# Two blocks of attention on one core: A's tokens transposed by DMA, weights on a second queue, eight heads accumulated at once

## The chip, the core and the metric

The kernel runs on one core of one Trainium2 chip. The metric is the time of one execution on the device in microseconds; where several executions are compared, their median. TensorE multiplies, VectorE and ScalarE read its results from PSUM (eight banks of 128 x 2 KB) and compute on them, GpSimd does small sums, and SyncE does nothing but issue DMAs. ScalarE can issue DMAs too; its queue is another one than SyncE's. In the profile, PE is TensorE's matmul, PEld its weight load, DVE VectorE, ACT ScalarE, POOL GpSimd, SP SyncE; a q behind an engine's name means its sequencer.

## The reference

Two independent problems A and B of the same shape, whose results stand side by side in the output. Each projects 16 x 32 tokens to 32 query heads, lets each group of eight heads attend to one of four cached key/value heads of 512 positions, and projects back:

```python
B, Sq, D = 16, 32, 1024
Hq, Hkv, Sk, Dh = 32, 4, 512, 128
q = (x @ wq).reshape(B, Sq, Hq, Dh).transpose(0, 2, 1, 3)
k = jnp.repeat(k_cache, Hq // Hkv, axis=1)
v = jnp.repeat(v_cache, Hq // Hkv, axis=1)
scores = jnp.einsum("bhqd,bhkd->bhqk", q, k) * (Dh ** -0.5)
o = jnp.einsum("bhqk,bhkd->bhqd", softmax(scores), v)
out = o.transpose(0, 2, 1, 3).reshape(B, Sq, Hq * Dh) @ wo
```

All inputs and outputs are bf16. x is 512 tokens by 1024, that is 1 MB; wq and wo are 8 MB each, and the keys and the values 8 MB each, for each problem.

## The kernel before

The kernel has a fast path, which holds all the time measured here, and a general path that is entered only when a check of the softmax sums fails. The fast path's order is written out by hand (a manual schedule): the program text gives the order on every engine and queue, and the framework adds the waits.

Everything follows 128 slots. A slot i is one pair of batch and key/value head: `scores(i)` (L357) makes four matmuls of a transposed key tile with eight heads' queries and an exponential on ScalarE, `partial_sums(i)` (L377) sums on VectorE, and five slots later `values(i)` (L424) multiplies with V and `normalize` (L438) writes the result. Between these TensorE works off `units` (L579), a stream of single matmuls: the query projections `q_units` (L299) of A's heads 8 to 31 and of all of B's, then the output projections `f_units` (L320). Each slot takes six or seven units.

The loads are issued by SyncE's queue in the order of the program. `load_k(j)` (L273) brings K for four slots as transposed tiles kT, with four DMA transposes of 128 KB for A and one of 512 KB for B; `load_v(j)` (L286) brings V for the same slots in one DMA of 512 KB; `load_wq(pr, c4)` (L246) brings the query weights of four heads, 1 MB, into a tile that it enters under (pr, c4) in the table `wq_tiles`, from which `q_units` takes it when a head begins. A plan (L583 to L603) says at which slot each load is issued. For the query weights it reads:

```python
for c4 in range(3, 16):
    need = (c4 - 2) * 4 * DC / 7.0
    at(max(0, int(need) - 10), load_wq, c4 // 8, c4 % 8)
```

so the tiles 3 and 4 are issued at slot 0, tile 5 at slot 3. At most eight DMAs of the two queues are outstanding on their eight semaphores: an issue waits for the DMA that used its semaphore before.

Ahead of the slots lies the projection of A's first eight heads, the part that the change is about (L460 to L561). SyncE loads x in five DMAs (`load_x`, tokens on partitions) and the weights of eight heads in eleven (`load_w0`), in turn. `transpose_x(k)` (L506) lets TensorE transpose two 128-column chunks of x through PSUM, and VectorE and ScalarE copy them to `xT`. `first_head` (L525) is one matmul of one head and one chunk of 128 columns. Six heads are accumulated chunk by chunk in six PSUM banks while the other two banks take the transposes; then the last two heads follow, each with its eight chunks in a row. `evacuate` (L534) copies a head to `qT`. A few matmuls on a zero tile (`warm_up`, L498) fill the time until the first data arrive. Behind them in SyncE's queue stand kT(0)'s first tile, wq(0,2), the rest of kT(0), V(0), kT(1) and V(1) (L489 to L494).

Of the kernel before, what the change touches and what calls it, by code (L numbers as in the profile page):

```python
# [8 lines left out]
BF16 = mybir.dt.bfloat16  # L9
FP32 = mybir.dt.float32  # L10
# [6 lines left out]
P = 128  # L17
HQ = 32
DH = 128
HKV = 4  # L20
REP = HQ // HKV
QD = 32
HALF = REP // 2
# [158 lines left out]
def kernel(  # L182
# [14 lines left out]
    nc = tc.nc  # L197
    B, SQ, D = A_x.shape
    SK = A_k_cache.shape[2]
    NTOK = B * SQ  # L200
    DC = D // P
    KC = SK // P
    TT = NTOK // P
    NOUT = D
    NW = 512
    NH = NOUT // NW
    GRP = 4
# [10 lines left out]
    def fast_path(ok_i):  # L218
        with ExitStack() as fctx:
            enter = fctx.enter_context  # L220
            const = enter(tc.tile_pool(name="const", bufs=1))
# [4 lines left out]
            psum = enter(tc.tile_pool(name="psum", bufs=2, space=bass.MemoryType.PSUM))  # L226
            enter(tc.manual_schedule())

            nc.scalar.preload_act_table_set("natural_log_exp_and_others")


            warm = work.tile([P, P], BF16, name="warm", tag="p_sb", bufs=7)
            nc.vector.memset(warm[:], 0.0)
            ident = const.tile([P, P], BF16, name="ident")
            make_identity(nc, ident[:])
            shift = const.tile([P, 1], FP32, name="shift")
            nc.vector.memset(shift[:], SHIFT)
            rall = const.tile([P, NG // 2, GRP * REP], FP32, name="rall")
# [2 lines left out]
            def blk_tile(shape, name, dtype=BF16):  # L241
                return blk.tile(shape, dtype, name=name, tag="blk")
# [3 lines left out]
            def load_wq(pr, c4, eng=None, parts=((0, 4),)):  # L246
                t = blk_tile([P, DC, 4 * DH], "wq_sb")
                v = problems[pr][3].rearrange("(c p) n -> p c n", p=P)
                for a, b in parts:
                    (eng or nc.sync).dma_start(  # L250
                        out=t[:, :, a * DH:b * DH],
                        in_=v[:, :, (c4 * 4 + a) * DH:(c4 * 4 + b) * DH],
                    )
                wq_tiles[pr, c4] = t
# [10 lines left out]
            def kv_part(j, which):  # L265
                pr, jj = divmod(j, NG // GRP)
                t = problems[pr][which]
                if pr == 0:
                    g, b0 = divmod(jj * GRP, B)
                    return t[b0:b0 + GRP, g]  # L270
                return t[jj]

            def load_k(j, qs=slice(0, GRP)):  # L273
                ks = kv_part(j, 1)
                if qs.start == 0:
                    k_tiles[j] = kv.tile([P, GRP, SK], BF16, name="kT")
                kT = k_tiles[j]
                if j < NG // GRP:
                    for q in range(qs.start, qs.stop):
                        nc.sync.dma_start_transpose(out=kT[:, q, :], in_=ks[q])  # L280
                else:
                    nc.sync.dma_start_transpose(
                        out=kT[:], in_=ks.rearrange("g k d -> (g k) d")
                    )

            def load_v(j):  # L286
                v_sb = v_tiles[j] = kv.tile([P, GRP, KC, DH], BF16, name="v_sb")
                nc.sync.dma_start(  # L288
                    out=v_sb[:],
                    in_=kv_part(j, 2).rearrange("q (p c) d -> p q c d", c=KC),  # L290
                )


            xT = [None, None]
            qT = {}
# [126 lines left out]
            ob = {}  # L422
# [34 lines left out]
                )  # L457


            x_sb = blk_tile([P, TT, D], "x_sb")  # L460
            x_v = A_x.flatten_outer_dims().rearrange("(t p) d -> p t d", p=P)
            wq_v = A_wq.rearrange("(c p) n -> p c n", p=P)
            HC = DC // 2
            w0 = [blk_tile([P, HC, REP * DH], "w0_sb") for _ in range(2)]

            def load_x(k, ts=slice(0, TT)):
                cs = slice(2 * k * P, (2 * k + 2) * P)
                nc.sync.dma_start(out=x_sb[:, ts, cs], in_=x_v[:, ts, cs])  # L468

            def load_w0(dcs, ns):  # L470
                nc.sync.dma_start(  # L471
                    out=w0[dcs.start // HC][:, dcs.start % HC:(dcs.stop - 1) % HC + 1, ns],
                    in_=wq_v[:, dcs, ns],
                )

            NF = REP - 2
            early, late = slice(0, NF * DH), slice(NF * DH, REP * DH)
            load_x(0, slice(0, TT // 2))
            load_x(0, slice(TT // 2, TT))
            load_w0(slice(0, 1), slice(0, NF * DH // 2))  # L480
            load_w0(slice(0, 1), slice(NF * DH // 2, NF * DH))
            load_w0(slice(1, 2), early)
            for k in range(1, DC // 2):
                load_x(k)
                load_w0(slice(2 * k, 2 * k + 1), early)
                load_w0(slice(2 * k + 1, 2 * k + 2), early)
            for half in (slice(0, HC), slice(HC, DC)):
                load_w0(half, late)
            load_k(0, slice(0, 1))  # L489
            load_wq(0, 2)  # L490
            load_k(0, slice(1, GRP))
            load_v(0)
            load_k(1)
            load_v(1)  # L494

            warm_ps = psum.tile([P, NW], FP32, name="warm_ps", tag="proj")

            def warm_up(n):  # L498
                for _ in range(n):
                    nc.tensor.matmul(  # L500
                        warm_ps[:, 0:P], lhsT=warm[:], rhs=warm[:], start=True, stop=True
                    )

            xT[0] = blk_tile([P, DC, NTOK], "xT")

            def transpose_x(k, fill=(0, 0)):  # L506
                ps = [
                    psum.tile([P, NTOK], BF16, name="xT_ps", tag="ob") for _ in range(2)
                ]
                for n, ts in zip(fill, (range(0, TT // 2), range(TT // 2, TT))):  # L510
                    for o in range(2):
                        dc = 2 * k + o
                        for tt in ts:
                            nc.tensor.transpose(  # L514
                                ps[o][:, tt * P:(tt + 1) * P],
                                x_sb[:, tt, dc * P:(dc + 1) * P],
                                ident[:],
                            )
                    warm_up(n)
                nc.vector.tensor_copy(out=xT[0][:, 2 * k, :], in_=ps[0][:])  # L520
                nc.scalar.copy(out=xT[0][:, 2 * k + 1, :], in_=ps[1][:])

            qT[0, 0] = blk_tile([P, B, REP, SQ], "qT")

            def first_head(q_ps, h, dc):  # L525
                nc.tensor.matmul(  # L526
                    q_ps,
                    lhsT=w0[dc // HC][:, dc % HC, h * DH:(h + 1) * DH],
                    rhs=xT[0][:, dc, :],
                    start=(dc == 0),  # L530
                    stop=(dc == DC - 1),
                )

            def evacuate(q_ps, h):  # L534
                copy = nc.vector.tensor_copy if h in (2, 1, 5, 7) else nc.scalar.copy
                copy(
                    out=qT[0, 0][:, :, h, :],
                    in_=q_ps.rearrange("p (b s) -> p b s", s=SQ),
                )

            warm_up(19)
            transpose_x(0, (2, 4))
            first_q = []
            for _ in range(2):
                pair_ps = psum.tile([P, 2, NW], FP32, name="q_ps", tag="s")
                first_q += [pair_ps[:, k, :] for k in range(2)]
            first_q += [psum.tile([P, NW], FP32, name="q_ps", tag="proj")[:] for _ in range(2)]
            for dc in range(DC - 2):
                for h in range(NF):
                    if dc % 2 and h == NF // 2:  # L550
                        transpose_x(dc // 2 + 1)
                    first_head(first_q[h], h, dc)
            for h in (0, 2, 4, 1, 3, 5):
                for dc in (DC - 2, DC - 1):
                    first_head(first_q[h], h, dc)
                evacuate(first_q[h], h)
            for h in range(NF, REP):
                q_ps = psum.tile([P, NW], FP32, name="q_ps", tag="ob")
                for dc in range(DC):
                    first_head(q_ps[:], h, dc)  # L560
                evacuate(q_ps[:], h)  # L561

            def stream():
                for h in range(REP, HQ):
# [20 lines left out]
            def at(slot, fn, *args):  # L585
                plan.setdefault(slot, []).append((fn, args))

            for j in range(2, 2 * NG // GRP):
                at(GRP * (j - 1), load_k, j)
                at(GRP * (j - 1) + 2, load_v, j)  # L590
            for c4 in range(3, 16):
                need = (c4 - 2) * 4 * DC / 7.0
                at(max(0, int(need) - 10), load_wq, c4 // 8, c4 % 8)
# [108 lines left out]
```

## Time and profile before

| | us |
|---|---|
| median of 14 runs | 346.93 |
| lowest and highest | 346.22, 348.57 |
| the profiled execution | 346.59 |
| its span, from first to last instruction | 344.8 |
| PE busy | 336.2 (98%) |
| DVE busy | 267.2 (78%) |
| ACT busy | 187.1 (54%) |
| A's first eight heads, first matmul to the next stage's first | 4.66 to 20.35 |
| first score matmul | 21.43 |

The granted TensorE clock is at full speed in all 40 slices of the span. The DMA engines moved 71.70 MB, 208 GB/s in the mean; 85% of sixteen engines' time went to SyncE's queue. A busy share is an average over stages, and a matmul's busy time includes what is pipelined under its neighbours, so the 98% of PE say little about a single stage; the chain of waits and the rows of single stretches do. A line of the chain gives a start, a length, and the engine and line, or the transfer, in which the time went. A line of a windows view gives a stretch, its length, for each engine the busy time and the number of instructions, then the granted clock, the share of the sixteen DMA engines (over 1 where packets of one engine overlap), and GB/s.

### The profile page before, as it was taken

What the parts mean: (1) busy time and instruction counts of PE and PEld (TensorE: products, weight loads), DVE (VectorE), ACT (ScalarE), POOL (GpSimd) and SP (SyncE); (2) the same over time, 40 slices, a digit from 0 to 9 for tenths busy, and PEclk for the clock granted to TensorE, in tenths of its full rate; (3) what the DMA queues carried; (4) which work ended last, traced back from release to release, by engine and by line L of the source; (5) the groups of instructions that cost most, each with busy time, mean ns of one, the idle gap of its engine ahead of it and who ended that gap; (6) DMA issues with size and microseconds to landing.
All of it is one profiled execution on the core that took longest, in us unless ns stands there. A gap on an engine that the chain in (4) does not pass through costs nothing.

```text
span 344.8 us, 5491 instructions
## 1 busy us (share of the span) xinstructions
PE 336.2 (98%) x2098; PEld 213.8 (62%) x2137; DVE 267.2 (78%) x338; ACT 187.1 (54%) x210; POOL 46.7 (14%) x206
## 2 busy tenths in 40 slices
PE   8997999999999999999999999999999999999996
PEld 5554666666666666666666666666666666666555
DVE  1236888888988898888888898889888888888540
ACT  2346667666676667666654545554455555554010
POOL 0001100111111111111002212221222100111100
PEclk9999999999999999999999999999999999999999
DMA  6999989899999988999999956999749997460001
GB/s 186 315 173 336 240 238 274 169 282 242 281 260 225 230 230 235 215 246 278 287 273 237 242 139 164 338 261 216 131 113 302 330 188 158 91 124 0 17 18 33
DMA packets 126509, 71.70 MB, mean 208 GB/s; under 512 B 73744, under 2 KB 126224, under 8 KB 126480
## 3 DMA queue, kind: packets, MB, share of 16 engines
q1 hardware_dynamic: 125952, 70.20, 85.3%
q0 software_dynamic: 384, 1.05, 0.8%
q8 instruction: 17, 0.28, 0.4%
q14 instruction: 12, 0.10, 0.1%
q10 hardware_dynamic: 144, 0.07, 0.1%
HBM read 51.38 MB, written 2.10 MB: 155 GB/s over the span
## 4 chain that ended last, share of the span: by engine, by line
PE 89%; SPq 5%; DMA 3%; issue 1%; ACT 0%; ACTq 0%
PE f_ps L325 31%; PE q_ps L306 25%; PE ob L430 17%; PE s_ps L362 16%; SPq L280 4%; DMA wq_sb<-in_A_wq_dram 2%; DMA x_sb<-in_A_x_dram 1%; SPq L471 1%; SPq L468 0%; SPq L288 0%; SPq L250 0%; ACT o_sb L334 0%; SPq L697 0%; ACTq L334 0%
## 5 line engine op out<-in xcount | busy, mean ns | idle before, releaser
L370 ACT ACTIVATE p_sb<-s_ps,shift 128x1024 bf16<-128x1024 f32 x128 | 142.7, 1115 | 103.3 <-PE s_ps L362 85.5
L381 DVE TRANSPOSE_TENSOR_REDUCE parts<-p_sb 128x32 f32<-128x1024 bf16 x128 | 158.9, 1242 | 20.8 <-ACT p_sb L370 19.1
L325 PE MATMUL f_ps<-wo_sb,oT 128*128 128x512 bf16 (+1 forms) x525 | 127.5, 366 | 0.5
L306 PE MATMUL q_ps<-xT,wq_sb 128*128 128x512 bf16 x430 | 113.7, 379 | 2.4 <-DMA wq_sb<-in_A_wq_dram 1.9
L430 PE MATMUL ob<-p_sb,v_sb 128*128 128x256 bf16 x512 | 76.8, 273 | 0.8
L362 PE MATMUL s_ps<-qT,kT 128*128 128x256 bf16 x512 | 76.8, 273 | 0.0
L325 PEld LDWEIGHTS <-oT 128*128 128x128 bf16 x544 | 53.2, 98 | 36.0
L362 PEld LDWEIGHTS <-kT 128*128 128x128 bf16 x512 | 56.8, 113 | 28.4 <-issue 0.3
L306 PEld LDWEIGHTS <-wq_sb 128*128 128x128 bf16 x448 | 43.7, 98 | 33.6 <-DMA wq_sb<-in_A_wq_dram 2.1
L430 PEld LDWEIGHTS <-v_sb 128*128 128x128 bf16 x512 | 50.1, 98 | 20.0
L452 DVE TENSOR_TENSOR oT<-r,ob 128x512 bf16<-128x512 f32 x64 | 43.9, 686 | 23.2 <-PE ob L430 22.7
L416 DVE STREAM_TRANSPOSE r<-rall 128x512 f32<-128x512 f32 x64 | 44.2, 691 | 1.1
L314 ACT CAST qT<-q_ps 128x512 bf16<-128x512 f32 x56 | 32.7, 583 | 13.8 <-PE q_ps L306 13.8
L399 POOL COPY half<-cs 64x32 f32<-64x32 f32 x32 | 6.5, 204 | 230.8 <-DVE cs L389 230.8
L334 ACT CAST o_sb<-f_ps 128x512 bf16<-128x512 f32 (+1 forms) x17 | 9.5, 559 | 24.4 <-PE f_ps L325 16.7
L526 PE MATMUL q_ps<-xT,w_sb 128*128 128x512 bf16 x62 | 14.4, 379 | 0.5 <-DVE xT L520 0.2
L389 DVE TENSOR_REDUCE cs<-parts 128x32 f32<-128x128 f32 x32 | 12.0, 376 | 1.1
L411 DVE RECIPROCAL rall<-sums 128x32 f32<-128x32 f32 x32 | 10.2, 320 | 1.6 <-POOL sums L408 1.6
L526 PEld LDWEIGHTS <-w_sb 128*128 128x128 bf16 x64 | 6.0, 98 | 7.4 <-DMA w_sb<-in_A_wq_dram 0.6
L520 DVE COPY xT<-xT_ps 128x512 bf16<-128x512 bf16 x4 | 1.7, 424 | 11.4 <-PE xT_ps L514 11.4
L336 POOL DMA_DIRECT2D out_dram<-o_sb x8 | 4.6, 574 | 33.2 <-ACT o_sb L334 33.1
L400 POOL TENSOR_TENSOR half<-half,cs 64x32 f32<-64x32 f32 x32 | 7.8, 243 | 2.6
(26 smaller groups left out, 50.8 us busy)
## 6 DMA issues: line engine op xcount, KB each, us to landing
v_sb<-in_A_v_cache_dram SPq DMA_DIRECT2D x16, 512.0 KB, 4.6
wq_sb<-in_B_wq_dram SPq DMA_DIRECT2D x8, 1024.0 KB, 6.3
wo_sb<-in_A_wo_dram SPq DMA_DIRECT2D x8, 1024.0 KB, 7.2
v_sb<-in_B_v_cache_dram SPq DMA_DIRECT2D x16, 512.0 KB, 4.7
wo_sb<-in_B_wo_dram SPq DMA_DIRECT2D x8, 1024.0 KB, 8.5
wq_sb<-in_A_wq_dram SPq DMA_DIRECT2D x6, 1024.0 KB, 7.6
w_sb<-in_A_wq_dram SPq DMA_DIRECT2D x7, 192.0 KB, 4.8
kT<-in_A_k_cache_dram SPq DMA_TRANSPOSE x64, 4.5
```

The source lines that it names most:

```text
L280: nc.sync.dma_start_transpose(out=kT[:, q, :], in_=ks[q])
L306: nc.tensor.matmul(ps[:], lhsT=w[:, dc, (h % 4) * DH:(h % 4 + 1) * DH], rhs=xT[pr][:, dc, :], start=(dc == 0), stop=(dc == DC - 1),)
L314: nc.scalar.copy(out=qT[pr, g][:, :, hl, :], in_=ps[:].rearrange("p (b s) -> p b s", s=SQ),)
L325: nc.tensor.matmul(ps[:, 0:width], lhsT=oT[pr, tt][:, h, :], rhs=wo_tiles[pr, nh, h // REP][:, h % REP, off:off + width], start=(h == 0), ...
L362: nc.tensor.matmul(s_ps[:, c, :], lhsT=kT[:, i % GRP, c, :], rhs=qT[pr, g][:, b, :, :].rearrange("p h s -> p (h s)"), start=True, stop=True,)
L370: nc.scalar.activation(out=p_sb[:], in_=s_ps[:], func=ACTF.Exp, bias=shift[:], scale=SCALE)
L381: nc.vector.tensor_reduce(out=parts[k][:, q, :, :].rearrange("p c h -> p (c h)"), in_=st[i]["p"][:].rearrange("p c (h s) -> p (c h) s", s=SQ),
L389: nc.vector.tensor_reduce(out=cs[:], in_=parts.pop(k)[:].rearrange("p q c h -> p q h c"), axis=AX.X, op=ALU.add,)
L416: nc.vector.transpose(out=r[:].rearrange("p n s -> p (n s)"), in_=rall[:, k, o * 2 * REP:(o + 1) * 2 * REP] .unsqueeze(2).to_broadcast([P, ...
L430: nc.tensor.matmul(ob[j][:, q, :], lhsT=v_sb[:, i % GRP, c, :], rhs=st[i]["p"][:, c, :], start=(c == 0), stop=(c == KC - 1),)
L452: nc.vector.tensor_tensor(out=out, in0=rcp.pop(j)[:].rearrange("p (q h) s -> p q h s", h=REP), in1=ob.pop(j)[:].rearrange("p q (h s) -> p ...
L526: nc.tensor.matmul(q_ps, lhsT=w0[dc // HC][:, dc % HC, h * DH:(h + 1) * DH], rhs=xT[0][:, dc, :], start=(dc == 0), stop=(dc == DC - 1),)
```

## The change

- x of A is no longer loaded and transposed on TensorE: SyncE issues five DMA transposes that write `xT` directly, two of one 128-column chunk and three of two chunks.
- The weights of the first eight heads are loaded from ScalarE's queue in six DMAs, the last three of 512 KB each; wq(0,2) is issued there too, and ScalarE's table load stands behind them.
- All eight heads are accumulated chunk by chunk, in all eight PSUM banks; the last two chunks are done head by head, and VectorE and ScalarE copy the heads in turn.
- SyncE's queue holds, behind x: kT(0), wq(0,3), kT(1), V(0), V(1). The plan of the slots is unchanged for the weights (it starts at tile 3).
- V's tiles 2 to 5 are loaded in two halves each.
- The identity, the transposes, their copies and the x tile are gone; there are 22 warm-up matmuls in a row instead of 25 in three groups.

```diff
-            nc.scalar.preload_act_table_set("natural_log_exp_and_others")
-            ident = const.tile([P, P], BF16, name="ident")
-            make_identity(nc, ident[:])
...
-            def load_v(j):
+            def load_v(j, pieces=1):
                 v_sb = v_tiles[j] = kv.tile([P, GRP, KC, DH], BF16, name="v_sb")
...
+                v = kv_part(j, 2).rearrange("q (p c) d -> p q c d", c=KC)
+                for k in range(pieces):
+                    qs = slice(k * GRP // pieces, (k + 1) * GRP // pieces)
+                    nc.sync.dma_start(out=v_sb[:, qs], in_=v[:, qs])
...
+            def load_x(d0, d1):
+                nc.sync.dma_start_transpose(
+                    out=xT[0][:, d0:d1, :],
+                    in_=A_x.flatten_outer_dims()[:, d0 * P:d1 * P],
+                )
+
+            def load_w0(d0, d1, h0=0, h1=REP):
+                nc.scalar.dma_start(
+                    out=w0[d0 // HC][:, d0 % HC:(d1 - 1) % HC + 1, h0 * DH:h1 * DH],
+                    in_=wq_v[:, d0:d1, h0 * DH:h1 * DH],
+                )
+
+            load_x(0, 1)
+            load_w0(0, 1, 0, HALF)
+            load_w0(0, 1, HALF, REP)
+            load_x(1, 2)
+            load_w0(1, 2)
+            for d0 in range(2, DC, 2):
+                load_x(d0, d0 + 2)
+                load_w0(d0, d0 + 2)
+            load_wq(0, 2, nc.scalar)
+            nc.scalar.preload_act_table_set("natural_log_exp_and_others")
+            load_k(0)
+            load_wq(0, 3)
+            load_k(1)
             load_v(0)
-            load_k(1)
             load_v(1)
...
+            first_q = [psum.tile([P, NW], FP32, name="q_ps", tag="proj")[:] for _ in range(2)]
+            for _ in range(2):
+                pair_ps = psum.tile([P, 2, NW], FP32, name="q_ps", tag="s")
+                first_q += [pair_ps[:, k, :] for k in range(2)]
+            first_q += [psum.tile([P, NW], FP32, name="q_ps", tag="ob")[:] for _ in range(2)]
+
+            for _ in range(22):
...
+            for dc in range(DC - 2):
+                for h in range(REP):
+                    first_head(h, dc)
+            for n, h in enumerate((2, 4, 0, 3, 1, 5, 6, 7)):
+                for dc in (DC - 2, DC - 1):
+                    first_head(h, dc)
+                copy = nc.vector.tensor_copy if n % 2 else nc.scalar.copy
...
-                at(GRP * (j - 1) + 2, load_v, j)
+                at(GRP * (j - 1) + 2, load_v, j, 2 if j < 6 else 1)
```

More of the change, by code (lines that the diff above doesn't have):

```diff
@@ L284, in load_k @@
                     )
-            def load_v(j):
+            def load_v(j, pieces=1):
                 v_sb = v_tiles[j] = kv.tile([P, GRP, KC, DH], BF16, name="v_sb")
[L288 to L291, printed above, removed]
+                v = kv_part(j, 2).rearrange("q (p c) d -> p q c d", c=KC)
+                for k in range(pieces):
+                    qs = slice(k * GRP // pieces, (k + 1) * GRP // pieces)
+                    nc.sync.dma_start(out=v_sb[:, qs], in_=v[:, qs])
             xT = [None, None]
@@ L457, in normalize @@
                 )
-            x_sb = blk_tile([P, TT, D], "x_sb")
-            x_v = A_x.flatten_outer_dims().rearrange("(t p) d -> p t d", p=P)
-            wq_v = A_wq.rearrange("(c p) n -> p c n", p=P)
+            xT[0] = blk_tile([P, DC, NTOK], "xT")
+            qT[0, 0] = blk_tile([P, B, REP, SQ], "qT")
             HC = DC // 2
             w0 = [blk_tile([P, HC, REP * DH], "w0_sb") for _ in range(2)]
-            def load_x(k, ts=slice(0, TT)):
-                cs = slice(2 * k * P, (2 * k + 2) * P)
-                nc.sync.dma_start(out=x_sb[:, ts, cs], in_=x_v[:, ts, cs])
@@ L470, in load_w0 @@
[L470 to L473, printed above, removed]
-                )
[L476 to L491, printed above, removed]
+            wq_v = A_wq.rearrange("(c p) n -> p c n", p=P)
+            def load_x(d0, d1):
+                nc.sync.dma_start_transpose(
+                    out=xT[0][:, d0:d1, :],
+                    in_=A_x.flatten_outer_dims()[:, d0 * P:d1 * P],
+                )
@@ L492, in fast_path @@
+            load_wq(0, 2, nc.scalar)
[3 more added lines that the diff above has]
+            load_k(1)
             load_v(0)
-            load_k(1)
             load_v(1)
[L496 to L527, printed above, removed]
+            first_q = [psum.tile([P, NW], FP32, name="q_ps", tag="proj")[:] for _ in range(2)]
[3 more added lines that the diff above has]
+            first_q += [psum.tile([P, NW], FP32, name="q_ps", tag="ob")[:] for _ in range(2)]
@@ L528, in first_head @@
+            for _ in range(22):
+                nc.tensor.matmul(
+                    first_q[REP - 1][:, 0:P], lhsT=warm[:], rhs=warm[:], start=True, stop=True
+                )
+            def first_head(h, dc):
+                nc.tensor.matmul(
+                    first_q[h],
                     lhsT=w0[dc // HC][:, dc % HC, h * DH:(h + 1) * DH],
@@ L532, in first_head @@
                 )
-            def evacuate(q_ps, h):
-                copy = nc.vector.tensor_copy if h in (2, 1, 5, 7) else nc.scalar.copy
+            for dc in range(DC - 2):
[5 more added lines that the diff above has]
+                copy = nc.vector.tensor_copy if n % 2 else nc.scalar.copy
                 copy(
                     out=qT[0, 0][:, :, h, :],
-                    in_=q_ps.rearrange("p (b s) -> p b s", s=SQ),
+                    in_=first_q[h].rearrange("p (b s) -> p b s", s=SQ),
                 )
[L541 to L561, printed above, removed]
             def stream():
```

## The prediction

> **What bounds the kernel now.** I read the page first, then the waits of TensorE, the chain of waits up to 36 us, and the DMA windows of the first 31 us. The page's chain says that TensorE sets the time, but not everywhere:
>
> ```profile
> PE 89%; SPq 5%; DMA 3%; issue 1%; ACT 0%; ACTq 0%
> PE f_ps L325 31%; PE q_ps L306 25%; PE ob L430 17%; PE s_ps L362 16%; SPq L280 4%; DMA wq_sb<-in_A_wq_dram 2%; DMA x_sb<-in_A_x_dram 1%; SPq L471 1%; SPq L468 0%; SPq L288 0%; SPq L250 0%; ACT o_sb L334 0%; SPq L697 0%; ACTq L334 0%
> ```
>
> The 8% of queue and transfer lie at the start. TensorE's waits in the whole span are these three:
>
> ```profile
> PE q_ps L306 <- DMA wq_sb<-in_A_wq_dram: 1.9, 1, 1.9
> PE warm_ps L500 <- DVE shift L237: 1.1, 1, 1.1
> PE q_ps L526 <- DVE xT L520: 0.2, 1, 0.2
> ```
>
> So after the start there is one stall, 1.87 us, for a weight tile. The chain (start us, us, what) tells which:
>
> ```profile
> 4.82 4.76 DMA x_sb<-in_A_x_dram
> ...
> 9.59 1.32 SPq L280
> ...
> 22.54 1.26 SPq L280
> ...
> 24.47 6.96 DMA wq_sb<-in_A_wq_dram
> ...
> 31.48 1.69 PE q_ps L306 x7
> ```
>
> It is wq(0,3), the weights of heads 12 to 15: issued at 24.47, landed at 31.43, awaited by TensorE since 29.6. Before 31.43 the chain holds no TensorE work at all. It runs back through SyncE's queue: K's transposes, V, the first loads. After it TensorE has no other wait to the end. The end of the kernel therefore follows the landing of wq(0,3) one for one, and whatever happens in the first projection counts only as far as it moves that landing, or outlasts it.
>
> **The first projection, TensorE's side.** In before it runs from 4.66 to 20.35, 15.69 us: 64 matmuls at a spacing of 0.218 (L306 x7: 1.69 less the last one's 0.379, over six) are 14.0; 24 token transposes at 0.057 (eight in 0.62, the last 0.219) are 1.4; waits the rest. The change takes all 32 transposes off TensorE, with their eight PSUM copies (0.42 on VectorE, 0.59 on ScalarE) and the identity on GpSimd, which ran beside other work. The new first matmul needs x's first transposed chunk. Its nearest row is kT, the same 512x128 bf16: 2.8 us from issue to landing at the least, 5.2 in the median. From 0.86 that is 3.7 to 6.1; I take 4.2, since nothing but weights is queued ahead. The stage then ends at 4.2 + 14.0 = 18.2 (17.7 to 20.1), 2.2 us before 20.35. The later chunks come in time: a kT issue takes 1.26 to 1.32 on SyncE's queue, a pair of chunks some 1.7 (B's xT: 6.79 for eight), so the last pair is issued by about 9 and its matmuls start at 4.2 + 6 x 1.74 = 14.6.
>
> ScalarE issues seven loads at 0.43 to 0.58 and then its 1.28 us table load; the last load waits for x's chunks 4 and 5 (landing near 9), so all is over near 11, and the first PSUM copy is wanted near 15. Cost nothing; without that cover, a delay of ScalarE's copies. Of the copies in alternation (0.59 and 0.69 per 0.87 us of matmuls) none is late; the pairs that share a tile have 0.28 us to spare. Scores still start 1.08 us after the stage's last matmul. The shorter queue of warm-up matmuls (22 for 25) is hidden under the wait for the first loads.
>
> Unstalled, TensorE would ask for wq(0,3) at 18.2 + 9.25 = 27.4 (9.25 is 20.35 to 29.6). In before it asked at 29.6 and got it at 31.43. So the 2.2 us gained arrive in front of the same door. What opens it?
>
> **The door: bytes ahead of wq(0,3).** The instruction order of the changed kernel shows wq(0,3) loaded twice: once behind kT(0), once in slot 0, where the plan still starts at 3. The second load replaces the tile in the table, and heads 12 to 15 read the second one; no matmul reads the first. SyncE's queue now holds x, kT(0), the unread copy, kT(1), v(0), v(1), and only then the copy that is read. In before 7.3 MB land ahead of and with wq(0,3) (x 1, weights of eight heads 2, wq(0,2) 1, two kT, two v, itself 1, in 1.05 MB units); now 8.4 MB. The DMA rows for those 29 us (stretch, length, engines, granted clock, DMA share, GB/s):
>
> ```profile
> 2.00:6.00 4.00, 3.82 (x33) 2.70 (x30) 0.42 (x1) 0.69 (x2) 0.00 (x0) 1.00 0.81 223
> 6.00:13.00 7.00, 6.82 (x43) 3.45 (x44) 0.85 (x2) 1.17 (x2) 0.00 (x0) 1.00 1.04 313
> 13.00:14.00 1.00, 1.00 (x12) 0.66 (x11) 0.33 (x1) 0.22 (x1) 0.00 (x0) 1.00 1.54 187
> 14.00:17.00 3.00, 2.87 (x14) 1.36 (x14) 1.48 (x3) 1.87 (x4) 0.00 (x0) 1.00 1.07 323
> 17.00:19.00 2.00, 2.00 (x11) 0.88 (x9) 0.69 (x1) 0.43 (x2) 0.00 (x0) 1.00 1.71 114
> 19.00:23.00 4.00, 4.00 (x23) 2.02 (x21) 0.69 (x1) 1.34 (x2) 0.00 (x0) 1.00 1.13 276
> 23.00:26.00 3.00, 2.95 (x19) 1.83 (x19) 2.08 (x2) 2.29 (x5) 0.00 (x0) 1.00 0.45 78
> 26.00:31.00 5.00, 3.61 (x20) 1.94 (x19) 3.43 (x5) 4.35 (x5) 0.13 (x1) 1.00 1.05 335
> ```
>
> The engines are full except at the start (0.81) and from 23 to 26 (0.45, SyncE still busy issuing kT(1)); twice they are held without moving much, at 13 and at 17 to 19. On this basis the landing of the copy that is read shifts by:
> - the unread copy: +3.0. The three wq in a row land at 31.43, 34.44 and 37.48, 3.0 apart.
> - x through transposes instead of plain loads: plain, 256 KB each 0.86 apart, 1 MB is 3.4; transposed, queued kT land 0.47 to 0.5 apart (8 chunks: 3.8), B's xT moved at 201 to 291 GB/s (3.6 to 5.2). So +0.3 to +1.7; I take +0.8.
> - the half-empty stretch 23 to 26: a queue 3 us longer covers it, -1.65 (3 x 0.55). Not at all, if SyncE falls behind: 0.
> - the start: two queues issue at once, and six weight issues take the place of eleven; at best the missing 0.19 of 4 us, -0.75. I take -0.5.
> - the two held stretches: nothing in the change aims at them; 0. Missed altogether they would give 1 x (1 - 187/330) + 2 x (1 - 114/330) = 1.7 (330 being between the rows of 323 and 335); a third like the longer one would cost 1.3.
> Sum: 3.0 + 0.8 - 1.65 - 0.5 = +1.65, from 3.0 + 0.3 - 1.65 - 0.75 - 1.7 = -0.8 up to 3.0 + 1.7 + 1.3 = +6.0. wq(0,3) lands near 33.1, well past the 27.4 (or 29.3) at which it is asked for.
>
> On the price of transposes the trace and a page differ. The Trainium skill, "Advanced Engine Details and Errata", section "X-Bar Transpose (TRN2)", calls transpose DMAs as fast as regular ones and expects 350 to 400 GB/s; here a queue of kT moved at 275 GB/s (97.4 to 98.5 us) while plain weights moved at 342 (27 to 30). By the page the second term would be, as an estimate, -0.5, and the sum +0.35. Against the two queues stands "DMA: Bandwidth & Descriptors", section "Issuing engines are not separate DMA queues": all issuers share the same 16 DMA engines, and several only save issue time. By it the start term keeps its sign but can be no more than the issue share above.
>
> **Behind the door.** wq(0,4), wq(0,5) and kT(2) follow in the same order, so they shift with it; kT(2)'s first tile landed at 37.96 and was used at 39.72, 1.76 to spare, as before. V's tiles 2 to 5 come in two halves: four more issues at 0.53, 2.1 us on SyncE's queue, ahead of kT(3) to kT(6). Their least slack is slot 20's (landed 64.41, used 67.68), 3.3; 1.2 remains. Nothing waits for the v halves alone (v(1): landed 28.48, used 42.76).
>
> **The sum.** The profiled execution took 346.59 (span 344.8), 0.34 below the median of 346.93. 346.59 + 1.65 = 348.24, as a median 348.6. About 0.2% (0.7 us) can be told from no change.
>
> **Rivals.**
> - Not slower: the two queues fill the DMA engines so well that the extra megabyte is paid from stalls. It decides where the savings (23 to 26, the start, the held stretches) pass 3.8 us; at their full 4.1 against 3.3 of cost, wq(0,3) lands 0.8 earlier; with a start denser than in any row of before, up to 1.8: 345.1 to 346.2. For it: 7.3 MB at 335 GB/s would take 21.9 us where 29.4 were spent (2.0 to 31.4). Against: the held stretches fall among kT's transposes, which are kept, and five transposes are added. 0.15.
> - No change: costs and savings meet within 0.7 us, 346.2 to 347.6. 0.2.
> - Slower by more: transposes on one queue beside plain loads on the other hold each other up, as at 17 to 19 (114 GB/s), two or three times; or SyncE falls behind and 23 to 26 stays empty. +3 to +6: 350 to 353. No row shows a transpose beside another queue's megabytes. 0.2.
> - That the change doesn't do what it says is part of the forecast: one early weight load is never read. Read from the first copy, the landing would come at least 3.0 sooner.
>
> **Numbers.** Forecast +0.7 to +3: 0.45. Faster 0.15, same 0.2, slower 0.65. The range, 345.8 to 351.8, leaves out the best of the first rival and the worst of the third.
>
> **What would show it.** Right: one TensorE stall at L301 for wq_sb, ending near 33 after 4 to 5 us; first projection over near 18; no kT stall later; DMA full from 3 to 30. Wrong: the stall ends before 31.4; or it is gone and TensorE waits for x or kT(2); or the transposed chunks land over 2 us apart, and the projection ends after 22.

## The result, and the profile after

The changed kernel took 351.06 us in the median (350.1 to 353.2, ten executions); the kernel before took 347.27 (346.22 to 349.23, 47) in the same measurement. The ratio is 1.0111 [1.0090, 1.0132]: slower, by about 3.8 us. (Ratios here are of means over the executions, so they can differ a little from the quotient of two medians.) The profiled execution took 352.19, with a span of 350.4 against 344.8, 5.6 us more.

The page's chain of kernel after:

```profile
PE 88%; SPq 8%; DMA 2%; issue 1%; ACT 0%; ACTq 0%
PE f_ps L320 31%; PE q_ps L301 25%; PE ob L425 17%; PE s_ps L357 15%; SPq L275 3%; SPq L462 3%; DMA wq_sb<-in_A_wq_dram 2%; SPq L286 1%; SPq L245 0%; ACT o_sb L329 0%; SPq L655 0%; ACTq L329 0%
```

TensorE's shares are nearly those of before; what is not TensorE has grown, by SyncE's issues: L462 is `load_x`, now transposes, with 3% of 350 us. TensorE's waits in after (engine, tile, line, releaser: us, times, longest):

```profile
PE q_ps L501 <- DMA xT<-in_A_x_dram: 4.0, 3, 1.9
PE q_ps L301 <- DMA wq_sb<-in_A_wq_dram: 2.8, 1, 2.8
PE q_ps L496 <- DVE shift L232: 1.1, 1, 1.1
```

There is still one stall for a weight tile, and three new waits for x's transposed chunks. The chain of after up to 38 us (start us, us, what) shows through what it runs:

```profile
4.77 6.41 SPq L462
...
17.79 0.58 SPq L245
18.43 3.28 SPq L275
...
26.30 1.49 SPq L286
...
27.83 7.58 DMA wq_sb<-in_A_wq_dram
...
35.45 2.35 PE q_ps L301 x7
```

The door is the same: the copy of wq(0,3) that is read, issued at 27.83, landed at 35.41, 3.98 later than in before. Ahead of it lie the copy that nobody reads (17.79) and one issue of an x transpose that held SyncE's queue for 6.41 us. TensorE's timeline in after (start, length, instructions, and in brackets the idle time before them):

```profile
4.77 3.57 PE L501 MATMUL q_ps<-xT,w_sb 128*128 128x512 bf16 x8 [1.17 <-DMA xT<-in_A_x_dram]
10.23 1.89 PE L501 MATMUL q_ps<-xT,w_sb 128*128 128x512 bf16 x8 [1.89 <-DMA xT<-in_A_x_dram]
13.09 10.52 PE L501 MATMUL q_ps<-xT,w_sb 128*128 128x512 bf16 x47 [0.97 <-DMA xT<-in_A_x_dram]
...
32.10 0.60 PE L357 MATMUL s_ps<-qT,kT 128*128 128x256 bf16 x4
35.45 2.35 PE L301 MATMUL q_ps<-xT,wq_sb 128*128 128x512 bf16 x7 [2.75 <-DMA wq_sb<-in_A_wq_dram]
```

x's first chunk landed at 4.73, the second at 10.19, the next pair at 13.05. The first projection gave way to the next stage at 23.45; before did so at 20.35. The last row is the stall, and it also shows something new: seven matmuls took 2.35 us there, 1.69 in before. The windows of after (columns as in before) put that beside the bytes:

```profile
2.00:6.00 4.00, 2.83 (x19) 1.85 (x17) 0.00 (x0) 0.00 (x0) 0.00 (x0) 1.00 0.90 216
6.00:13.00 7.00, 4.23 (x14) 1.54 (x13) 0.00 (x0) 0.00 (x0) 0.00 (x0) 1.00 1.14 203
13.00:14.00 1.00, 0.91 (x5) 0.43 (x5) 0.00 (x0) 0.00 (x0) 0.00 (x0) 1.00 1.13 393
14.00:17.00 3.00, 2.95 (x15) 1.34 (x15) 0.00 (x0) 1.17 (x1) 0.00 (x0) 1.00 1.07 263
17.00:19.00 2.00, 2.00 (x11) 0.93 (x10) 0.00 (x0) 0.12 (x1) 0.00 (x0) 1.00 0.90 212
19.00:23.00 4.00, 4.00 (x20) 1.76 (x19) 1.60 (x3) 1.76 (x3) 0.00 (x0) 1.00 1.13 309
23.00:26.00 3.00, 2.99 (x16) 1.58 (x16) 1.17 (x2) 1.42 (x2) 0.00 (x0) 1.00 1.16 321
26.00:31.00 5.00, 4.96 (x29) 2.99 (x29) 3.29 (x3) 4.01 (x6) 0.00 (x0) 1.00 1.17 235
35.45:36.32 0.87, 0.86 (x4) 0.41 (x5) 0.73 (x2) 0.00 (x0) 0.07 (x1) 1.00 1.10 350
36.32:39.74 3.42, 3.20 (x13) 1.81 (x13) 0.33 (x1) 1.04 (x2) 0.00 (x0) 0.50 1.09 348
```

From 6 to 13 the DMA engines are busier than in before (1.14 against 1.04) and move less (203 GB/s against 313). The hole from 23 to 26 is filled. The last two rows lie behind the stall: the granted clock was full for another 0.87 us, and then 0.50 for 3.42 us. At half clock 3.42 us of time hold 1.7 us of work, so 1.7 us were lost there.

From the windows the landing can be booked. GB/s times us gives kB; 335 GB/s turns a difference into time, and the unread copy goes in at the 3.0 us by which the query weights of before land apart:

| stretch | before, MB | after, MB | us on the landing |
|---|---|---|---|
| 2 to 13 (223x4 + 313x7; 216x4 + 203x7) | 3.08 | 2.29 | +2.4 |
| 13 to 23 | 2.49 | 2.84 | -1.1 |
| 23 to 26 | 0.23 | 0.96 | -2.2 |
| 26 to 31 | 1.68 | 1.18 | +1.5 |
| the unread copy, 1.05 MB more | | | +3.0 |

The sum is +3.6; +3.98 was measured. That leaves 5.6 - 3.98 = 1.6 us of the longer span, behind the landing; the 1.7 us lost at half clock account for it.

### The profile page after: what moved, and what is told of

It is laid out like the page before. It is cut to its first block, busy times and chain, and to the rows that moved or that the text cites. A ratio compares the mean times of both kernels' runs of the same rounds, so it can differ in the third digit from the quotient of the medians.

```text
span 350.4 us, 5409 instructions
## 1 busy us (share of the span) xinstructions
PE 337.2 (96%) x2063; PEld 212.8 (61%) x2102; DVE 265.6 (76%) x334; ACT 184.8 (53%) x206; POOL 46.2 (13%) x204
## 3 DMA queue, kind: packets, MB, share of 16 engines
q0 software_dynamic: 384, 1.05, 0.8%
## 4 chain that ended last, share of the span: by engine, by line
PE 88%; SPq 8%; DMA 2%; issue 1%; ACT 0%; ACTq 0%
PE f_ps L320 31%; PE q_ps L301 25%; PE ob L425 17%; PE s_ps L357 15%; SPq L275 3%; SPq L462 3%; DMA wq_sb<-in_A_wq_dram 2%; SPq L286 1%; SPq L245 0%; ACT o_sb L329 0%; SPq L655 0%; ACTq L329 0%
## 5 line engine op out<-in xcount | busy, mean ns | idle before, releaser
L501 PE MATMUL q_ps<-xT,w_sb 128*128 128x512 bf16 x63 | 15.9, 410 | 4.1 <-DMA xT<-in_A_x_dram 4.0
L516 DVE CAST qT<-q_ps 128x512 bf16<-128x512 f32 x4 | 2.8, 692 | 20.5 <-PE q_ps L501 20.4
L482 ACT ACT_TABLE_LOAD x1 | 1.3, 1283 | 15.8 <-DMA xT<-in_A_x_dram 15.8
```

Of the source, the lines that this page charges most:

```text
L501: nc.tensor.matmul(first_q[h], lhsT=w0[dc // HC][:, dc % HC, h * DH:(h + 1) * DH], rhs=xT[0][:, dc, :], start=(dc == 0), stop=(dc == DC - 1),)
```

## The experiments

Two theories were on the table. One: the end follows the landing of the copy of wq(0,3) that is read, the unread copy costs about 3 us of it, and x by transposes costs the rest. The rival: the two queues, or the transposes themselves, are the cost, and the unread megabyte is mostly hidden. The runs, with the medians of the kernel before on the same chip:

| run | median us | before | ratio and 95% interval |
|---|---|---|---|
| e1_one_copy | 347.55 | 346.72 | 1.0021 [1.0001, 1.0042] |
| e2_before_extra_copy | 350.11 | 346.72 | 1.0107 [1.0053, 1.0161] |
| e3_one_queue | 353.45 | 346.72 | 1.0191 [1.0147, 1.0236] |
| e4_one_queue_one_copy | 346.73 | 346.72 | 0.9991 [0.9971, 1.0012] |
| e5_before_early_wq3 | 344.76 | 346.78 | 0.9929 [0.9903, 0.9955] |
| e6_extra_copy_filled | 348.73 | 346.78 | 1.0036 [1.0010, 1.0061] |
| e7_x_in_two_groups | 345.16 | 346.78 | 0.9947 [0.9920, 0.9973] |
| e8_after_filled | 352.98 | 346.87 | 1.0170 [1.0135, 1.0205] |
| e9_two_groups_two_queues | 349.14 | 346.87 | 1.0031 [1.0000, 1.0062] |

**One copy instead of two (e1).** After, with the plan's loads from 4 on, so that the early copy is the one that is read:

```diff
-            for c4 in range(3, 16):
+            for c4 in range(4, 16):
```

> The changed kernel, with the plan starting at tile 4, so that wq(0,3) is loaded once and heads 12 to 15 read the early copy. Theory (the second copy's place in the queue sets the stall, and x's slow transposes set the rest): the stall for wq_sb near 33 us is gone, since the early copy landed at 25.5 in the changed kernel and is asked for at 32.7. TensorE is then late by the first projection's end alone, 23.45 against 20.35 + 1.87 in the kernel before, +1.2 us, and the half-clock stretch after the long stall goes too: about 348.4. Rival one (the extra megabyte was paid from empty stretches and the slow x is everything): no more than 0.5 us off the changed kernel, about 350.5. Rival two (the two queues are no loss, the second copy is the whole of it): as fast as the kernel before or faster, 345 to 347.

347.55 against 351.06: without the unread copy only 0.2% is left of the 1.1%. The stall for wq_sb is gone from the waits of e1:

```profile
PE q_ps L501 <- DMA xT<-in_A_x_dram: 3.0, 2, 1.8
PE q_ps L496 <- DVE shift L232: 1.1, 1, 1.1
```

The tile landed at 25.30, and the chain of e1 is TensorE's for 96%. So most of the loss goes with the second copy, and the first projection, which ends later than in before, now sets the end. But the edit does two things: it takes the extra bytes out, and it lets heads 12 to 15 read the early copy, by which the stall of 1.87 us that before has itself goes too. e2 and e5 below take the two apart. The profiled execution, at 349.48 the longest of the ten, had another trouble in the first projection (the timeline's row, then a row of the windows):

```profile
10.16 15.19 PE L501 MATMUL q_ps<-xT,w_sb 128*128 128x512 bf16 x55 [1.78 <-DMA xT<-in_A_x_dram]
```

```profile
10.16:16.10 5.94, 5.93 (x15) 2.02 (x15) 0.00 (x0) 0.26 (x1) 0.00 (x0) 1.00 1.13 251
```

From 10.16 on, 55 matmuls took 15.19 us; up to 16.1 they stood 0.43 apart, twice the 0.218 of before, and the projection ended at 25.19, 1.7 later than in after. The granted clock in the row is 1.00 all the same. So this figure does not show every slow stretch, and an execution with a mean clock near 1 can hold one. In after the first eight matmuls (3.57 us from 4.77) are as far apart; there TensorE waits for the next chunk in any case.

**The extra copy alone (e2).** Before, with the second load and nothing else:

```diff
             load_k(0, slice(1, GRP))
+            load_wq(0, 3)
```

> The kernel before, with one more load of wq(0,3) behind kT(0) that no matmul reads; the plan still loads the tile again at slot 0. Theory: the copy that is read lands 3.0 us later, less up to 1.65 of the half-empty stretch from 23 to 26, so +1.35 (to +3.0) in its landing and in the time: 348.6 (to 350.2). Rival (copies are hidden by the empty stretches): no change, 347.3. If the time rises by more than 3.5, the stall has a price beyond its length, such as a half clock after it.

The copy that is read landed at 32.82, 1.39 later than in before, where 3.0 - 1.65 = 1.35 had been forecast. The sum is right, with some luck in its parts: the hole from 23 to 26 (324 GB/s in e2 against 78) gave back 2.2 us for the 1.65, and from 26 to 31 the engines moved 285 GB/s instead of 335, which took 0.7 again. But the kernel lost 3.4 us, not 1.4. The two rows of e2 that show where, the timeline's first and then the windows':

```profile
32.86 2.98 PE L306 MATMUL q_ps<-xT,wq_sb 128*128 128x512 bf16 x7 [3.13 <-DMA wq_sb<-in_A_wq_dram]
```

```profile
33.10:36.51 3.41, 3.41 (x12) 1.52 (x11) 0.67 (x1) 0.00 (x0) 0.00 (x0) 0.50 1.09 349
```

The stall has grown from 1.87 to 3.13 us, and just behind it TensorE runs for 3.41 us at a granted clock of 0.50, as long as in after. All four executions of e2 show it in their mean clock (0.990 to 0.995). Its price can be read from the kernel before itself: of 62 executions beside e1 to e9, 49 had a mean clock of 0.998 or more and a median of 346.72, and 13 had 0.993 to 0.995 and a median of 348.76. That is 2.0 us, and 1.4 + 2.0 is e2's 3.4. That those 13 lost their clock behind the stall of 1.87 us is argued, not shown: no profile fell on one of them. What speaks for it is that a wait of 1.92 us was enough in the profile of e7, and that none of nine executions lost clock in e5, where the stall is gone.

**The stall filled (e6).** e2 with 50 small matmuls on the zero tile ahead of head 12, in that head's PSUM bank, before its first real matmul overwrites it:

```diff
+                if (pr, h) == (0, 12):
+                    for _ in range(50):
+                        nc.tensor.matmul(
+                            ps[:, 0:P], lhsT=warm[:], rhs=warm[:], start=True, stop=True
+                        )
```

> The kernel before with the unread extra copy (350.1 us, stall 3.1 us, then 3.4 us at half clock), and with 50 matmuls of the zero tile ahead of head 12's first, 2.8 us of work at 0.056 each, which fill the stall. Theory (a stall over some 3 us makes TensorE run at half clock for 3.4 us behind it, 1.7 us lost): the clock stays full, the stall for wq_sb is 0.3 us, and the time falls to 346.7 + 1.4 = 348.1 to 348.4. Rival (the half clock comes from something else in this order, or costs nothing): 350.

In the timeline of e6 the filler takes the place of the stall:

```profile
30.03 2.96 PE L307 MATMUL q_ps<-warm 128*128 128x128 bf16 x50
33.32 1.68 PE L311 MATMUL q_ps<-xT,wq_sb 128*128 128x512 bf16 x7 [0.34 <-DMA wq_sb<-in_A_wq_dram]
```

Seven matmuls take 1.68 us again, the mean clock was 0.998 or more in all ten executions, and the median fell by 1.4 us against e2 although the weights landed 0.45 later (33.27), which also puts 348.73 above the forecast 348.1 to 348.4. This settles the second term: in this kernel the idle time costs more than its own length.

**The early load without the second one (e5).** Before, with wq(0,3) behind kT(0) and the plan from 4 on:

```diff
             load_k(0, slice(1, GRP))
+            load_wq(0, 3)
...
-            for c4 in range(3, 16):
+            for c4 in range(4, 16):
```

> The kernel before, with wq(0,3) loaded once, behind kT(0) instead of at slot 0. Theory (the end follows the landing of the tile that is read): in the run with the extra copy this early load landed at 24.2 and heads 12 to 15 ask at 29.7, so the 1.87 us stall goes and nothing takes its place: 346.7 - 1.9 = 344.9, a ratio of 0.9946. Rival (the loads behind it, V and K, come 3 us later and stall TensorE instead): no change, 346.7, with a wait for kT or v_sb.

344.76, faster than both kernels and as forecast. The waits of e5:

```profile
PE warm_ps L501 <- DVE shift L237: 1.1, 1, 1.1
PE q_ps L527 <- DMA w_sb<-in_A_wq_dram: 0.3, 1, 0.3
```

wq(0,3) landed at 24.32, more than 5 us before it was wanted, and from 23 to 26 the engines moved 328 GB/s. The chain is TensorE's for 97%, and none of nine executions fell below a mean clock of 0.999. The whole of the door is worth 2.0 us. Against the 18 of 26 executions of before that kept their clock (median 346.59) it is 1.8, the stall of 1.87; the rest is the clock.

**One queue (e3, e4).** After with `nc.sync` in place of `nc.scalar` for the first weights and wq(0,2); e3 keeps both copies, e4 one (the edit of e1):

```diff
-                nc.scalar.dma_start(
+                nc.sync.dma_start(
...
-            load_wq(0, 2, nc.scalar)
+            load_wq(0, 2)
```

> The changed kernel with the weights of the first eight heads and wq(0,2) on SyncE's queue too, in the same order of issue; the second copy stays. Theory (transposes and plain loads of two queues hold each other up: x's second chunk landed 8.05 us after its issue): on one queue the chunks land in order, each pair by 12 to 14 us, the first projection ends near 19.5 to 20.5, and the copy of wq(0,3) that is read lands near 33, 2 us earlier than in the changed kernel: 348.7 to 349.2. Rival (transposes of x are slow by themselves, for their 256-byte rows 2 KB apart): chunks as late as before, first projection to 23, 350.5 to 351.5.

> Both edits: one queue, and wq(0,3) loaded once, early. Theory: no stall for wq_sb, first projection over near 19.5 to 20.5 against 22.2 (20.35 + 1.87) in the kernel before: 344.6 to 345.6, faster than both kernels. Rival (x's transposes slow by themselves): first projection to 23, about 348. Rival two (the next load in line, kT(2), has only 1.8 us to spare and stalls TensorE once wq(0,3) does not): 346.5 to 347.5 with a wait for kT.

The forecasts for both missed: they held the second queue to be what slows the transposes. Only the second rival of e4 names its time, 346.5 to 347.5 with a wait for kT. The windows from 2 to 13 us, of after, e3 and e4 in turn:

```profile
2.00:13.00 11.00, 7.07 (x32) 3.39 (x30) 0.00 (x0) 0.00 (x0) 0.00 (x0) 1.00 1.05 208
```

```profile
2.00:13.00 11.00, 8.39 (x38) 3.67 (x36) 0.00 (x0) 0.10 (x1) 0.00 (x0) 1.00 0.89 194
```

```profile
2.00:13.00 11.00, 9.15 (x38) 3.82 (x36) 0.00 (x0) 0.10 (x1) 0.00 (x0) 1.00 0.88 193
```

Before moved 281 GB/s there. Transposes and plain loads in turn are as slow on one queue as on two. Part of it on one queue is the start, where SyncE issues everything: from 2 to 6 the DMA share was 0.58 in e3 and 0.55 in e4. From 6 to 13 the engines were full (1.07 in both) and moved 219 and 220 GB/s, against 313 in before. In e3 the copy that is read landed at 35.37, no earlier than in after, but the projection ended sooner (22.20), so the stall was longer, 3.96 us, and all four executions lost clock, three of them with a mean of 0.990, which is twice the loss of one such stretch; where it lies was not seen, since the profile fell on the fourth. That is how a kernel with a quicker front came out behind after. e4, with no stall for wq_sb and a full mean clock, equals before: its projection ends at 22.27, and 20.35 + 1.87 = 22.22 is where before stands once its stall is paid. The wait for kT is there too, but short: the chain of e4 runs through kT(2)'s landing at 40.08, for which TensorE's weight load waited 0.64 us. The matmuls around it, at a spacing of 0.218, lost about 0.3 by it (an estimate), and 344.8 + 0.05 + 0.3 comes to about the span of e4, 345.1.

**x in two groups (e7, e9).** x comes in two transposes of four chunks, each ahead of four weight loads; one copy of wq(0,3); e7 issues all from SyncE, e9 keeps the weights on ScalarE's queue. The warm-up is 48 matmuls long.

```diff
-            load_x(0, 1)
...
-            for d0 in range(2, DC, 2):
-                load_x(d0, d0 + 2)
-                load_w0(d0, d0 + 2)
+            for d0 in (0, HC):
+                load_x(d0, d0 + HC)
+                for d in range(d0, d0 + HC):
+                    load_w0(d, d + 1)
...
-            for _ in range(22):
+            for _ in range(48):
...
-            for c4 in range(3, 16):
+            for c4 in range(4, 16):
```

e7 also has the edit of e4, `nc.sync` for `nc.scalar`.

> One queue and one copy of wq(0,3), but x in two DMA transposes of four chunks, each followed by its four weight chunks in single loads, and 48 warm-up matmuls instead of 22. Theory (a transpose next to plain loads, on one queue or two, costs at each change from one kind to the other): three changes instead of nine, 2 to 13 us move 250 to 290 GB/s instead of 193, the first projection ends near 20 to 20.8 instead of 22.3: 344.7 to 345.3. Rival (it is the bytes in 256-byte rows that are slow, however ordered): 2 to 13 us at about 200 GB/s, the projection to 22 or later, 346.5 or more.

> The kernel with x in two groups of four chunks and one copy of wq(0,3) (345.16 us), with the eight weight loads and wq(0,2) on ScalarE's queue: so the transposes lie beside plain loads of another queue again, as in the change. Theory (side by side they slow each other, on whichever queue; the order in groups was the cure): 2 to 13 us move about 210 GB/s instead of 249, x's first group lands 3 us or more later than 5.2, the projection ends 1 to 3 us later, 346 to 348. Rival (only the number of changes from one kind to the other counts, or the two queues are free): 344.7 to 345.3.

The same windows of e7, then e9:

```profile
2.00:13.00 11.00, 9.08 (x61) 5.53 (x59) 0.00 (x0) 0.10 (x1) 0.00 (x0) 0.84 0.98 249
```

```profile
2.00:13.00 11.00, 6.98 (x51) 4.66 (x49) 0.00 (x0) 0.93 (x1) 0.00 (x0) 0.77 1.14 222
```

Grouped on one queue the front moves 249 GB/s in place of 193, and e7 takes 345.16, as forecast. That is faster than before, but not than e5 (344.76), which leaves x to TensorE. With the weights on the other queue the same order moves 222; x's first group landed at 9.51 instead of 5.17, and TensorE waited 4.0 us for it. So both count: the order in groups, and the second queue beside a transpose. What in the grouping helps, fewer changes of kind or fewer and larger transposes, was not taken apart. The profile of e7 fell on one of the two of its ten executions that lost clock (347.20 and 347.26, mean 0.995), and shows behind which wait:

```profile
7.40 15.67 PE L497 MATMUL q_ps<-xT,w_sb 128*128 128x512 bf16 x64 [1.92 <-DMA w_sb<-in_A_wq_dram]
```

```profile
7.77:11.18 3.41, 3.41 (x10) 1.22 (x8) 0.00 (x0) 0.00 (x0) 0.00 (x0) 0.50 1.15 241
```

Three executions of e9 at a full mean clock took 346.3 to 346.9, inside its forecast of 346 to 348; the seven others (0.990 to 0.995) took 348.4 to 350.1 and put the median above it. The window of e9, with its clock of 0.77, is from one of the latter, with a mean of 0.990: there the clock was 0.50 in one piece from 7.89 to 14.71, twice 3.41 us. The Trainium skill, "DMA: Bandwidth & Descriptors", section "Issuing engines are not separate DMA queues", has a second issuer save issue time alone; here it saved nothing (e1 against e4: 347.55 and 346.73) or cost (e9 against e7).

**After with its stall filled (e8).** After with 45 of the matmuls of e6 ahead of head 12:

```diff
+                if (pr, h) == (0, 12):
+                    for _ in range(45):
...
```

> The changed kernel with 45 matmuls of the zero tile (2.5 us) ahead of head 12's first, in the 2.75 us in which it waits for the second copy of wq(0,3). Nothing else moves. Theory (part of the 3.8 us is a half clock behind the stall, in about half of the executions): the clock is full at the tile's landing, the slow executions at 352 to 353 go, and the median falls by 0.5 to 1.7 us: 349.4 to 350.5. Rival (the landing is the whole of it): no change, 351.

The expectation missed: 352.98, no better than after. The waits hold no wq_sb, and four of six executions kept their clock, but in the profile the weights landed at 37.01, 1.6 later than in after. Why it moved is open: V(0), two loads ahead, took 6.36 us to land, and from 26 to 31 the engines moved 261 GB/s. Nor did the end follow that landing alone. The filler ran to 37.23, 0.2 behind it, and the chain is TensorE's for 96%, from x's second chunk on:

```profile
2.14 8.28 DMA xT<-in_A_x_dram
10.42 0.04 issue
10.46 15.17 PE q_ps L506 x56
...
34.72 2.51 PE q_ps L302 x45
37.23 1.51 PE q_ps L306 x7
```

This is the slow first projection of e1's profile once more: 56 matmuls in 15.17 us, over at 25.47, 2.0 later than in after, while the execution's mean clock is 1.00. With TensorE at head 12 that late, the filler lay in its way. Whether the other five executions had the same front was not seen. This run is no clean test of the clock term; e6 is.

## Why the prediction was right or wrong

**Right: the door.** The end followed the landing of wq(0,3) in the kernels that kept the second copy: +1.39 in e2, +1.84 in e6, +3.94 in e3 and +3.98 in after, with the clock term on top where there was one. Only in e8 did TensorE itself come as late as the tile. What an earlier first projection saves buys nothing, as argued: e3's ends 1.25 before that of after, and the tile lands at the same time.

**Right: the unread copy.** The +3.0 less what the hole takes came out in e2 at 1.39 for 1.35, though the hole gave back 2.2 for the 1.65 and a later stretch took the difference. By itself the copy costs the kernel before 3.4 us, nearly the 3.8 of the whole change. The early load as such is good, which e5 shows by leaving the second one out.

**Wrong in size: x by transposes, and the start with two queues.** The sum had +0.8 and -0.5; to 13 us the two together cost 2.4. The term took its rate from rows where transposes stood in a queue among themselves (0.47 to 0.5 us a chunk). In the change they alternate with plain loads, and there the chunks landed at 4.73, 10.19 and 13.05: the sign that the prediction had named as wrong, chunks over 2 us apart and a projection over after 22, came true (23.45 for 18.2). "The later chunks come in time" was worked from issue lengths of 1.3 to 1.7; one issue took 6.41, and the second chunk landed 8.05 after its issue. ScalarE's loads were not over near 11 either but at 15.8, and its table load at 17.1; that cost nothing, as the first copy came at 20.6.

**Wrong in size: the held stretches.** Booked at nothing, they did not stay where they were: 13 to 23 gave 1.1 back, and 26 to 31, full in before, cost 1.5. Together +0.4, so the zero was not far off, but by luck of two signs.

**Missing: the clock.** The sum let a longer stall cost its own length. In the profile of after a stall of 2.75 us was followed by 3.42 us at a granted clock of 0.50. Of twelve executions of after five kept a mean clock of 0.999 or more, with a median of 350.48, and seven (0.994 to 0.995) did not, with a median of 352.19. The stall itself was forecast too long and too early ("4 to 5 us, ending near 33"): it was 2.75 and ended at 35.41, since the projection that asks for the tile was late as well. The shorter queue of warm-up matmuls was booked at nothing too; in the profiles of e1 and e8 the first projection ran at half pace to about 16, behind these 22. That the shorter queue is the cause was not tested.

**The rivals.** The measured +3.8 is more than twice the sum's +1.65 and above the +0.7 to +3 that was thought likeliest; it lies in the range of the third rival, slower by more. That rival's mechanism is there, though wider than it was put: the transposes and plain loads hold each other up on one queue too. What that front costs depends on the door. Behind the unread copy it adds little (after +3.8, e2 +3.4). With one early copy it costs 2.8 us, 347.55 in e1 for 344.76 in e5, of which only 0.8 shows against before, as before has its own stall to pay. V's halves and the new order of V and kT(1) were not run by themselves; in no profile does TensorE wait for V.

**The rule on transposes.** The Trainium skill, "Advanced Engine Details and Errata", section "X-Bar Transpose (TRN2)", calls transposes as fast as regular loads. In no front measured here were they: 193 to 249 GB/s in total with them, 281 without. These are totals over all loads in flight; no run times x's transposes by themselves.

## What to carry to other kernels

Look for what the chain waits on before making the stage ahead of it faster: a quicker front before the same door only lengthens the stall, and a stall of 2 to 3 us can cost another 1.7 us in TensorE's clock. When a load is moved forward by hand, take it out of the plan that also issues it: the load alone made this kernel 0.7% faster, twice it made it 1% slower. If a load must be a DMA transpose, put the transposes in groups, apart from plain loads on another queue; here that came within 0.4 us of leaving the transposes to TensorE (e7 and e5), not below. And don't expect the DMA share to tell: from 6 to 13 in after it was 1.14, at the lowest rate of its rows.

## What the runs showed of the hardware that was not expected

- Behind waits of 1.92 us (e7), 2.75 (after), 3.13 (e2) and 3.96 (e3) TensorE's granted clock was 0.50 for 3.41 to 3.42 us, beginning 0.2 to 0.9 us after the wait was over. That loses 1.7 us; executions with and without it differ by 1.7 (after) to 2.2 us (e7). 50 matmuls of 0.06 us in the stall removed it. The Trainium skill, "TensorE: Matmul & The Clock Gate", section "Part 1: The HAM clock gate (the "warmup" mystery)", gives an idle window of about 3.4 us for the gate to close and as much to open it. The second agrees with the 3.41; for the first, 1.92 us was enough here, in the one profile of e7.
- The granted clock does not show every slow stretch: in e1 it reads 1.00 from 10.16 to 16.10, where matmuls stood 0.43 apart instead of 0.218.
- x's transposes beside weight loads: 128 KB took 8.05 us from issue to landing, with SyncE held 6.41 us in one issue. Total rates from 2 to 13 us: 193 and 208 GB/s in turn (one queue, two queues), 249 and 222 in groups, 281 with plain loads alone. What in the chip makes the difference was not settled.
